# A fused attention and feed-forward kernel: batch 0 loaded on one queue with its values cast on chip, and its first feed-forward units cut by token part

## The chip, the cores and the metric

The kernel runs on one core of a Trainium2 chip. A core has five engines that run their own instruction lists and wait for each other by semaphores: TensorE (PE; its weight loads are shown as PEld), VectorE (DVE), ScalarE (ACT), GpSimd (POOL) and SyncE (SP), which here only issues DMAs. Sixteen DMA engines move the data that the queues of SP, POOL and ACT ask for. The metric is the device time of one execution in microseconds (us).

## The reference

For q, k, v of shape 8 batches x 8 heads x 576 tokens x 64, in float32:

```python
q_s = exp(q - max(q, -1));  q_s /= sum(q_s, -1)        # softmax over the 64 features
k_s = exp(k - max(k, 2));   k_s /= sum(k_s, 2)         # softmax over the 576 tokens
kv  = einsum('bhsd,bhse->bhde', k_s, v)                # 64 x 64 per head
x   = einsum('bhsd,bhde->bhse', q_s, kv)               # -> 4608 rows of 512
g   = x @ w_gate;  u = x @ w_val                       # 512 -> 1536
out = (silu(g) * u) @ w_out                            # 1536 -> 512, float32
```

## The kernel before

**Tiling.** Heads go in two groups G of four (`NG`). One load (`load`, L72) brings a group of q, k or v of one batch as a float32 tile of 128 partitions x 2 x 576 (576 KB). A partition holds nine tokens (`T` = 9) of 64 features, so a group of queries is nine slices t of 64 tokens; `BANKS` cuts them into a part a (t 0 to 4, 320 tokens) and a part b (t 5 to 8, 256 tokens). In what follows "01a" is batch 0, group 1, part a.

**Attention of a group.** ACT takes exponentials of q and k (`exp_of`: tiles `eq`, `ek`). DVE sums the rows of `eq` (`norm_sum`: `rs`, then the reciprocal `rr`) and multiplies (`norm_mul`: `qs`). PE transposes `qs` (`turn_pe`: `tp`), and ACT or DVE copies the result out of PSUM (`turn_out`: `qt`). PE sums the exponentials of the keys over the tokens (`key_sum`: `ks`; DVE takes the reciprocal `kvr`) and multiplies them with the values (`kv_first`: `kv`). ACT or DVE scales that by `kvr` (`scale_first`: `kn`). PE multiplies `qt` with `kn` (`x_mm`: `xp`), and ACT and DVE copy it into the bfloat16 tile `xt` (`x_out`), which the feed-forward part reads. For batch 0 the values arrive in bfloat16 (`v16`): the DMA itself casts them. The later batches are loaded in float32 and cast by GpSimd (`cast_v`).

**Feed-forward.** Twelve units m of 128 columns of `w_gate` and `w_val` (`m_unit`, L286): per unit eight matmuls for gate and eight for value in batch 0, as its 576 tokens are two parts of 320 and 256 columns; ACT applies silu (`sg`), DVE multiplies (`hr`). Output units (`o_mm`, L322) then multiply 128 tokens of `hr` with `w_out`. Batch 0 is fed forward alone, while the loads of batch 1 are awaited; from then on attention of batch b is laid between units of the chunk before it.

**Order of the work.** All engines' orders are written by hand (`manual_schedule`): an engine takes its instructions in the order of the program text. The queue of SP issues the loads of q and k of batch 0, in the order q0, k0, q1, k1. The queue of POOL issues, once k0 has landed, v0, v1 in two pieces, and then the weights in column slices (0 to 256, 256 to 640, 640 to 1024, 1024 to 1536; gate and value in turn, cast from float32 to bfloat16 on the way; `w_slice`, L99) and four slices of `w_out` (`wo_slice`, L107). At most eight DMAs of POOL's queue are outstanding: an issue waits for the one eight before it. The loads of batch 1 (`load_batch`) wait until the second slice of `w_out` has landed. `spin` (L388) runs matmuls on zeros whose result nobody reads, which keep TensorE busy ahead of the real work. `bank` gives out the eight PSUM banks in turn.

**The start, in program order on PE:** 8 spins, 6 spins after the first `rs`, ks0, tp00a, tp00b, 6 spins, ks1, kv0, tp01a, tp01b, x 00a, x 00b, kv1, x 01a, x 01b, and the twelve units, of which the first (`by_part`) does all matmuls of its part of 320 columns before those of 256.

Of the kernel before, what the change touches and what calls it, by code (L numbers as in the profile page):

```python
# [8 lines left out]
FP32 = mybir.dt.float32  # L9
BF16 = mybir.dt.bfloat16  # L10
AF = mybir.ActivationFunctionType
# [4 lines left out]
def kernel(  # L16
# [10 lines left out]
    nc = tc.nc  # L27
# [6 lines left out]
    T = S // 64  # L34
# [12 lines left out]
    def bank(name):  # L47
        return psp.tile([128, 512], FP32, tag="ps", name=name)
# [13 lines left out]

    raw = {}

    def head_ap(src, b, G, t0=0, t1=T):
        return bass.AP(
            tensor=src.tensor,
            offset=src[b, 4 * G].offset + 64 * t0,
            ap=[[T * 64, 128], [2 * HSTR, 2], [1, (t1 - t0) * 64]],
        )  # L70

    def load(what, src, b, G, pieces=((0, T),), after=None):  # L72
        t_ = ld.tile([128, 2, T * 64], FP32, tag=what, name=what)
        raw[what, b, G] = t_
        last = None
        for t0, t1 in pieces:
            last = nc.sync.dma_start(out=t_[:, :, 64 * t0:64 * t1], in_=head_ap(src, b, G, t0, t1))
            if after is not None:
                tc.add_manual_dep(last.ins, after.ins.name, SYNC, reason="order of loads")
                after = None  # L80
        return last
# [37 lines left out]
    def exp_of(what, b, G, pieces=((0, T),)):  # L119
        s = st.setdefault((b, G), {})  # L120
        e = s["e" + what] = at.tile([128, T, 2, 64], BF16, tag="e" + what, name="e" + what)
        src = raw[what, b, G].rearrange("p h (t d) -> p t h d", d=64)
        for t0, t1 in pieces:
            nc.scalar.activation(out=e[:, t0:t1], in_=src[:, t0:t1], func=AF.Exp)  # L124

    def cast_v(b, G):
        nc.gpsimd.tensor_copy(  # L127
# [4 lines left out]
    def norm_sum(b, G, pieces=((0, T),)):  # L132
        s = st[b, G]
        eq2 = s["eq"].rearrange("p t h d -> p (t h) d")
        rs = at.tile([128, 2 * T], FP32, tag="rs", name="rs")
        first = None
        for t0, t1 in pieces:
            i = nc.vector.reduce_sum(  # L138
                out=rs[:, 2 * t0:2 * t1], in_=eq2[:, 2 * t0:2 * t1, :], axis=mybir.AxisListType.X
            )  # L140
            first = first or i
        rr = s["rr"] = at.tile([128, 2 * T], FP32, tag="rr", name="rr")
        nc.vector.reciprocal(out=rr, in_=rs)
        return first

    def norm_mul(b, G, pieces=((0, T),), engs=None):
        s = st[b, G]
        eq2 = s["eq"].rearrange("p t h d -> p (t h) d")
        qs = s["qs"] = at.tile([128, T, 128], BF16, tag="qs", name="qs")
        for (t0, t1), eng in zip(pieces, engs or (nc.vector, nc.vector)):  # L150
            n = 2 * (t1 - t0)
            eng.tensor_mul(  # L152
                qs[:, t0:t1, :].rearrange("p t (h d) -> p (t h) d", d=64),
                eq2[:, 2 * t0:2 * t1, :],
                s["rr"][:, 2 * t0:2 * t1].to_broadcast([128, n, 64]),
            )
# [126 lines left out]

    def m_unit(c0, n, m, by_part=False):  # L286
        ms = slice(m * 128, (m + 1) * 128)
        parts = [(c0, n)] if n <= 512 else [(c0, 320), (c0 + 320, n - 320)]
        gu = []
        for nm in ("g_ps", "u_ps"):  # L290
            ps = [bank(nm) for _ in parts]
            gu.append(ps)
        steps = [(a, kk, i) for a in range(2) for kk in range(KT) for i in range(len(parts))]
        if by_part:
            steps.sort(key=lambda a: (a[2], a[0], a[1]))
        for a, kk, i in steps:
            c, w_ = parts[i]
            nc.tensor.matmul(  # L298
                out=gu[a][i][:, 0:w_], lhsT=(wg, wv)[a][:, kk, ms], rhs=xt[:, kk, c:c + w_],
                start=(kk == 0), stop=(kk == KT - 1),  # L300
            )
        for g_ps, u_ps, (c, w_) in zip(gu[0], gu[1], parts):
            r = c % RING
            sg = ff.tile([128, 512], BF16, tag="sg", name="sg")
            nc.scalar.activation(out=sg[:, 0:w_], in_=g_ps[:, 0:w_], func=AF.Silu)  # L305
            nc.vector.tensor_mul(hr[:, m, r:r + w_], sg[:, 0:w_], u_ps[:, 0:w_])  # L306

    def store(j, o_sb, c0=0, c1=512, engs=(nc.sync, nc.sync)):
        for half in range(2):
# [41 lines left out]

    make_identity(nc, ident)
    with tc.manual_schedule():
        kd = []
        for G in range(NG):
            load("q", q, 0, G)
            kd.append(load("k", k, 0, G))
        d = nc.gpsimd.dma_start(out=v16[0], in_=head_ap(v, 0, 0))
        tc.add_manual_dep(d.ins, kd[0].ins.name, SYNC, reason="order of loads")
        for t0, t1 in BANKS:  # L360
            nc.gpsimd.dma_start(out=v16[1][:, :, 64 * t0:64 * t1], in_=head_ap(v, 0, 1, t0, t1))  # L361

        warm = const.tile([128, 1], FP32, name="warm", tag="warm")
        nc.vector.memset(warm, 0.0)
# [5 lines left out]
        for vb in vbs:  # L370
            nc.vector.memset(vb[:, :, 128:129], 1.0)

        exp_of("q", 0, 0, BANKS)
        exp_of("k", 0, 0)
        exp_of("q", 0, 1, BANKS)
        first = norm_sum(0, 0, BANKS)
        norm_mul(0, 0, BANKS)
        norm_sum(0, 1, BANKS)

        for c0, n in ((0, 256), (256, 384), (640, 384), (1024, 512)):  # L380
            w_slice(wg, moe_w_gate, c0, n)
            w_slice(wv, moe_w_val, c0, n)
        w_dma = [wo_slice(m0, 3) for m0 in (0, 3, 6, 9)]

        def spin(n, after=None):
            idle = bank("idle")
            for _ in range(n):
                i = nc.tensor.matmul(out=idle, lhsT=zero[:, 0:128], rhs=zero, start=True, stop=True)  # L388
                if after is not None:
                    tc.add_manual_dep(i.ins, after.ins.name, SYNC, reason="start of the warm-up")  # L390
                    after = None

        def key_sum(G):
            s = st[0, G]
            ks = bank("ks")
            for t in range(T):
                nc.tensor.matmul(
                    out=ks[:, 0:2], lhsT=s["ek"][:, t, :, :].rearrange("p h d -> p (h d)"), rhs=sel,
                    start=(t == 0), stop=(t == T - 1),
                )  # L400
            s["kvr"] = at.tile([128, 2], FP32, tag="kvr", name="kvr")
            nc.vector.reciprocal(out=s["kvr"], in_=ks[:, 0:2])

        def kv_first(G, t0=0, t1=T):
            s = st[0, G]
            if t0 == 0:
                s["kv"] = [bank("kv") for _ in range(2)]
            for t in range(t0, t1):
                for g in range(2):
                    r = slice(64 * g, 64 * g + 64)  # L410
                    nc.tensor.matmul(
                        out=s["kv"][g][:, 0:128].rearrange("p (h d) -> p h d", d=64),
                        lhsT=ek_of(0, G, g, t), rhs=v16[G][r, :, 64 * t:64 * t + 64],
                        start=(t == 0), stop=(t == T - 1),
                    )

        def scale_first(G, eng1):
            s = st[0, G]
            kn = s["kn"] = at.tile([128, 2, 128], BF16, tag="kn1", name="kn1")
            nc.scalar.mul(kn[:, 0, :], s["kv"][0][:, 0:128], s["kvr"][:, 0:1])  # L420
            if eng1 is nc.scalar:
                nc.scalar.mul(kn[:, 1, :], s["kv"][1][:, 0:128], s["kvr"][:, 1:2])
            else:
                nc.vector.tensor_scalar_mul(kn[:, 1, :], s["kv"][1][:, 0:128], s["kvr"][:, 1:2])

        spin(8)
        spin(6, first)
        key_sum(0)
        turn_pe(0, 0, 0)
        turn_pe(0, 0, 1)  # L430
        turn_out(0, 0, 0, nc.scalar)
        exp_of("k", 0, 1)
        turn_out(0, 0, 1, nc.scalar)
        norm_mul(0, 1, BANKS)
        spin(6)
        key_sum(1)
        kv_first(0)
        scale_first(0, nc.scalar)
        turn_pe(0, 1, 0)
        turn_pe(0, 1, 1)  # L440
        turn_out(0, 1, 0, nc.vector)
        turn_out(0, 1, 1, nc.vector)
        xp0 = x_mm(0, 0, 0), x_mm(0, 0, 1)
        kv_first(1, *BANKS[0])
        kv_first(1, *BANKS[1])
        x_out(0, 0, 0, xp0[0], (nc.scalar, nc.scalar))
        x_out(0, 0, 1, xp0[1], (nc.vector, None))
        scale_first(1, nc.vector)
        xp1 = x_mm(0, 1, 0), x_mm(0, 1, 1)
        x_out(0, 1, 0, xp1[0], (nc.scalar, nc.vector))  # L450
        x_out(0, 0, 1, xp0[1], (None, nc.vector))
        x_out(0, 1, 1, xp1[1], (nc.scalar, nc.vector))

        load_batch(1, w_dma[-3], by_group=True)
        load_batch(2)

        for m in range(MT):
            m_unit(0, S, m, by_part=(m == 0))

        exp_of("q", 1, 0)  # L460
        exp_of("k", 1, 0)
# [121 lines left out]
```

The softmax here doesn't subtract the row's maximum and nothing guards it: scores larger than these inputs give would overflow.

## Time and profile before

| what | value |
|---|---|
| median of 7 runs | 317.46 us (317.23 to 317.70) |
| the profiled execution, its own time | 318.08 us |
| its span, from the first to the last event of the profile | 316.3 us |
| PE busy | 305.8 us (97% of the span) |
| DVE, ACT, POOL busy | 162.9, 147.4, 28.0 us |
| first feed-forward matmul of batch 0 | 14.90 us |
| first output matmul (end of batch 0's units) | 39.60 us |
| mean DMA rate over the span | 145 GB/s |

Times in the traces count from the start of the span. "Busy" of PE is modelled and includes pipelined waiting inside a matmul. The DMA rates count a casting transfer by the bytes that it writes, so the weights, read as float32 and written as bfloat16, show half of what is read. An engine's idle time matters only where it is on the chain that ends last. Nearly all of PE's idle time at the start lies ahead of the first feed-forward matmul and in the first units.

### The profile page before, as it was taken

The numbers are of one execution on the slowest core, as the hardware profiler recorded it, in microseconds if no ns is written. First come the engines' busy times: TensorE is split into PE (matmuls) and PEld (weight loads), VectorE is DVE, ScalarE is ACT, GpSimd is POOL, SyncE is SP. The second block draws the span as 40 slices with busy tenths as digits, with TensorE's granted clock in tenths as the row PEclk, the third lists the DMA queues.
The fourth block names the chain that finished last, engine by engine and source line by source line (L and its number), as shares of the span: only waits on it lengthen the run. The fifth ranks groups of instructions, "written<-read, shape, count | busy, mean of one in ns | idle before, by whom it ended". The sixth has DMA issues, their size and how long they took to land.

```text
span 316.3 us, 4856 instructions
## 1 busy us (share of the span) xinstructions
PE 305.8 (97%) x1865; PEld 152.8 (48%) x1894; DVE 162.9 (52%) x277; ACT 147.4 (47%) x218; POOL 28.0 (9%) x35
## 2 busy tenths in 40 slices
PE   5999999999999999999999999999999999999994
PEld 2577744554445444544454444544454444444443
DVE  3834476685764567455835492639354333423421
ACT  4743397634763465447364647355733113312300
POOL 2920021101100020002000200020000000000000
PEclk9899999999999999999999999999999999999998
DMA  7999999169246906490629253944310202020124
GB/s 270 188 203 207 300 394 390 55 149 373 47 96 168 348 13 132 102 393 21 141 66 347 103 108 69 314 170 102 64 43 0 64 4 66 0 68 3 31 68 102
DMA packets 39304, 45.75 MB, mean 145 GB/s; under 512 B 16368, under 2 KB 23024, under 8 KB 39280
## 3 DMA queue, kind: packets, MB, share of 16 engines
q1 hardware_dynamic: 32480, 39.99, 42.1%
q0 software_dynamic: 6640, 5.31, 10.9%
q8 instruction: 15, 0.25, 0.3%
q10 hardware_dynamic: 160, 0.13, 0.2%
q14 instruction: 9, 0.07, 0.1%
HBM read 37.75 MB, written 9.44 MB: 149 GB/s over the span
## 4 chain that ended last, share of the span: by engine, by line
PE 87%; DMA 5%; DVE 3%; ACT 2%; POOL 1%; issue 1%; SPq 0%; DVEq 0%
PE g_ps L298 28%; PE u_ps L298 28%; PE o_ps L322 25%; DMA wv<-in_moe_w_val_dram 3%; PE kv L191 3%; DMA k<-in_k_dram 2%; DVE rs L138 1%; PE xp L267 1%; DVE qs L152 1%; PE o_ps L342 1%; ACT L124 1%; ACT eq L124 1%; POOL wg L99 0%; POOL v L361 0%; PE tp L166 0%
## 5 line engine op out<-in xcount | busy, mean ns | idle before, releaser
L305 ACT ACTIVATE sg<-g_ps 128x512 bf16<-128x512 f32 (+2 forms) x120 | 65.0, 554 | 139.5 <-PE g_ps L298 120.0
L306 DVE TENSOR_TENSOR hr<-sg,u_ps 128x512 bf16<-128x512 bf16 (+2 forms) x120 | 74.4, 630 | 88.1 <-PE u_ps L298 80.7
L298 PE MATMUL g_ps<-xt,wg 128*128 128x512 bf16 (+2 forms) x469 | 110.0, 357 | 1.0 <-ACT xt L111 0.2
L298 PE MATMUL u_ps<-xt,wv 128*128 128x512 bf16 (+2 forms) x468 | 109.7, 357 | 1.3 <-DMA wv<-in_moe_w_val_dram 0.6
L322 PE MATMUL o_ps<-wo,hr 128*128 128x512 bf16 x414 | 93.0, 379 | 0.4 <-issue 0.2
L298 PEld LDWEIGHTS <-wv 128*128 128x128 bf16 x480 | 46.8, 98 | 47.5 <-DMA wv<-in_moe_w_val_dram 1.3
L298 PEld LDWEIGHTS <-wg 128*128 128x128 bf16 x480 | 45.8, 98 | 45.2 <-issue 1.1
L322 PEld LDWEIGHTS <-hr 128*128 128x128 bf16 x420 | 40.9, 98 | 49.1
L113 DVE COPY o_sb<-o_ps 128x512 f32<-128x512 f32 x33 | 22.4, 680 | 39.2 <-PE o_ps L322 37.3
L127 POOL CAST vb<-v 128x1152 bf16<-128x1152 f32 x14 | 16.0, 1146 | 173.7 <-DMA v<-in_v_dram 166.4
L138 DVE TENSOR_REDUCE rs<-eq 128x18 f32<-128x1152 bf16 (+2 forms) x18 | 21.7, 1214 | 13.0 <-ACT eq L124 13.0
L152 DVE TENSOR_TENSOR qs<-eq,rr 128x1152 bf16<-128x1152 bf16 (+2 forms) x18 | 22.0, 1231 | 0.1
L124 ACT ACTIVATE eq<-q 128x1152 bf16<-128x1152 f32 (+2 forms) x18 | 18.2, 1053 | 4.1 <-DMA q<-in_q_dram 4.0
L124 ACT ACTIVATE ek<-k 128x1152 bf16<-128x1152 f32 x16 | 18.0, 1159 | 0.3 <-DMA k<-in_k_dram 0.2
L305 ACT ACT_TABLE_LOAD x12 | 15.4, 1283 | 0.2
L124 ACT ACT_TABLE_LOAD x11 | 14.1, 1283 | 0.2
L388 PE MATMUL idle<-zero 128*128 128x512 bf16 x20 | 7.3, 526 | 3.2 <-DVE rs L138 2.0
L191 PE MATMUL kv<-vb,ek 64*128 64x129 bf16 x252 | 8.7, 217 | 0.0
L191 PEld LDWEIGHTS <-ek 64*128 64x128 bf16 x252 | 7.3, 94 | 2.7 <-ACT sg L305 2.1
L275 ACT CAST xt<-xp 128x512 bf16<-128x512 f32 x12 | 6.4, 588 | 3.6 <-PE xp L267 3.6
L276 DVE CAST xt<-xp 128x512 bf16<-128x512 f32 x12 | 7.7, 682 | 0.0
L347 ACT COPY o_sb<-o_ps 128x128 f32<-128x128 f32 x2 | 0.5, 266 | 13.3 <-DVE o_sb L346 13.3
(46 smaller groups left out, 71.5 us busy)
## 6 DMA issues: line engine op xcount, KB each, us to landing
q<-in_q_dram SPq DMA_DIRECT2D x16, 576.0 KB, 5.4
k<-in_k_dram SPq DMA_DIRECT2D x16, 576.0 KB, 7.2
out_dram<-o_sb SPq DMA_DIRECT2D x70, 128.0 KB, 2.3
v<-in_v_dram SPq DMA_DIRECT2D x14, 576.0 KB, 8.7
wo<-in_moe_w_out_dram POOLq DMA_DIRECT2D x4, 384.0 KB, 16.7
wg<-in_moe_w_gate_dram POOLq DMA_DIRECT2D x2, 384.0 KB, 10.0
wv<-in_moe_w_val_dram POOLq DMA_DIRECT2D x2, 384.0 KB, 11.1
wg<-in_moe_w_gate_dram POOLq DMA_DIRECT2D x1, 512.0 KB, 14.1
```

What stands on the lines that cost most here:

```text
L113: eng.tensor_copy(out=out, in_=in_)
L124: nc.scalar.activation(out=e[:, t0:t1], in_=src[:, t0:t1], func=AF.Exp)
L127: nc.gpsimd.tensor_copy(out=vbs[G][:, :, 0:128].rearrange("p t (h d) -> p t h d", d=64), in_=raw["v", b, G].rearrange("p h (t d) -> p t h ...
L138: i = nc.vector.reduce_sum(out=rs[:, 2 * t0:2 * t1], in_=eq2[:, 2 * t0:2 * t1, :], axis=mybir.AxisListType.X)
L152: eng.tensor_mul(qs[:, t0:t1, :].rearrange("p t (h d) -> p (t h) d", d=64), eq2[:, 2 * t0:2 * t1, :], s["rr"][:, 2 * t0:2 * t1].to_broadca ...
L191: nc.tensor.matmul(out=kv[g][:, c:c + 129], lhsT=ek_of(b, G, g, t), rhs=vbs[G][r, t, 0:129], start=(t == 0), stop=(t == T - 1),)
L276: nc.vector.tensor_copy(out=xt[:, 2 * G + 1, c0:c0 + 512], in_=main[G][1])
L298: nc.tensor.matmul(out=gu[a][i][:, 0:w_], lhsT=(wg, wv)[a][:, kk, ms], rhs=xt[:, kk, c:c + w_], start=(kk == 0), stop=(kk == KT - 1),)
L305: nc.scalar.activation(out=sg[:, 0:w_], in_=g_ps[:, 0:w_], func=AF.Silu)
L306: nc.vector.tensor_mul(hr[:, m, r:r + w_], sg[:, 0:w_], u_ps[:, 0:w_])
L322: nc.tensor.matmul(out=o_ps, lhsT=hr[:, m, r0:r0 + 128], rhs=wo[:, m, :], start=(m == 0), stop=(m == MT - 1),)
L388: i = nc.tensor.matmul(out=idle, lhsT=zero[:, 0:128], rhs=zero, start=True, stop=True)
```

## The change

- **Loads.** All six loads of batch 0 go to SP's queue in float32, in the order q0, k0, q1, v0, k1, v1, and the first weight DMA waits for v0 in place of v waiting for k0. POOL issues no loads of values.
- **Values** are cast on chip into `v16`: group 0 whole by ACT, group 1 by POOL (t 0 to 2), DVE (t 3 to 5) and ACT (t 6 to 8). POOL's cast stands in its queue between the issue of `wg` 128 to 384 and that of `wv` 128 to 384.
- **Weight slices** are 0 to 128, 128 to 384, 384 to 768, 768 to 1152 and 1152 to 1536: ten DMAs in place of eight, for the same bytes.
- **Query normalization** is done part by part (`norm_part`: sum, reciprocal, product), and part 01b is left until the feed-forward has begun.
- **Key sums of group 1** are taken in two parts, and ACT's exponentials of k1 come in two pieces, after the cast of v0. The scaling of `kv` is done by DVE twice for group 0, and by ACT and DVE for group 1.
- **The first three units** are split by `m_part` and `m_out`: matmuls of units 0, 1 and 2 on the first 320 tokens, with tp01b after unit 1 and x 01b after unit 2, and then of units 0, 1, 2 on the other 256.
- **Spins:** 10, and three times 3, tied to the first exponential, the first row sum and the first reciprocal; 3 more before tp00b and 6 before tp01a.

```diff
-        kd = []
-        for G in range(NG):
-            load("q", q, 0, G)
-            kd.append(load("k", k, 0, G))
-        d = nc.gpsimd.dma_start(out=v16[0], in_=head_ap(v, 0, 0))
-        tc.add_manual_dep(d.ins, kd[0].ins.name, SYNC, reason="order of loads")
-        for t0, t1 in BANKS:
-            nc.gpsimd.dma_start(out=v16[1][:, :, 64 * t0:64 * t1], in_=head_ap(v, 0, 1, t0, t1))
+        for what, src, G in (("q", q, 0), ("k", k, 0), ("q", q, 1), ("v", v, 0), ("k", k, 1), ("v", v, 1)):
+            d = load(what, src, 0, G)
+            if (what, G) == ("v", 0):
+                v_dma = d
...
+        steps += norm_part(0, 0)
+        norm_part(0, 1)
+        def cast_part(G, eng, t0, t1):
+            c = slice(64 * t0, 64 * t1)
+            copy(eng, v16[G][:, :, c], raw["v", 0, G][:, :, c])
+        w0 = w_slice(wg, moe_w_gate, 0, 128)
+        tc.add_manual_dep(w0.ins, v_dma.ins.name, SYNC, reason="order of loads")
+        w_slice(wv, moe_w_val, 0, 128)
+        w_slice(wg, moe_w_gate, 128, 256)
+        cast_part(1, nc.gpsimd, 0, 3)
+        w_slice(wv, moe_w_val, 128, 256)
-        for c0, n in ((0, 256), (256, 384), (640, 384), (1024, 512)):
+        for c0, n in ((384, 384), (768, 384), (1152, 384)):
...
-        spin(8)
-        spin(6, first)
-        key_sum(0)
-        turn_pe(0, 0, 0)
+        spin(10)
+        for i in (0, 2, 3):
+            spin(3, steps[i])
+        turn_pe(0, 0, 0)
+        turn_out(0, 0, 0, nc.scalar)
+        exp_of("q", 0, 1, BANKS)
+        key_sum(0)
+        spin(3)
         turn_pe(0, 0, 1)
-        turn_out(0, 0, 0, nc.scalar)
-        exp_of("k", 0, 1)
         turn_out(0, 0, 1, nc.scalar)
-        norm_mul(0, 1, BANKS)
+        norm_part(1, 0)
+        cast_part(0, nc.scalar, 0, T)
         spin(6)
-        key_sum(1)
+        turn_pe(0, 1, 0)
+        turn_out(0, 1, 0, nc.vector)
+        exp_of("k", 0, 1, BANKS)
+        key_rec(0)
         kv_first(0)
-        scale_first(0, nc.scalar)
...
+        scale_first(0, (nc.vector, nc.vector))
+        key_sum(1, *BANKS[0])
+        cast_part(1, nc.vector, 3, 6)
+        cast_part(1, nc.scalar, 6, T)
+        xp = x_mm(0, 0, 0)
+        key_sum(1, *BANKS[1])
+        kv_first(1)
+        x_out(0, 0, 0, xp)
+        key_rec(1)
+        scale_first(1, (nc.scalar, nc.vector))
+        xp = x_mm(0, 1, 0), x_mm(0, 0, 1)
+        x_out(0, 1, 0, xp[0])
+        x_out(0, 0, 1, xp[1])
+        half = (0, 320), (320, S - 320)
+        units = [m_part(0, half[:1], m) for m in range(2)]
+        norm_part(1, 1)
         turn_pe(0, 1, 1)
+        units.append(m_part(0, half[:1], 2))
+        m_out(units[0])
         turn_out(0, 1, 1, nc.vector)
...
+        m_out(units[1])
+        x_out(0, 1, 1, x_mm(0, 1, 1))
+        m_out(units[2])
+        for m in range(3):
+            m_out(m_part(0, half[1:], m))
...
-        for m in range(MT):
-            m_unit(0, S, m, by_part=(m == 0))
+        for m in range(3, MT):
+            m_unit(0, S, m)
```

## The prediction

> **What bounds the kernel now.** The page's chain by engine comes first, then the chain in order of time, the timeline of the first 40 us, and the busy time by stretches for DMA and clock.
>
> ```profile
> PE 87%; DMA 5%; DVE 3%; ACT 2%; POOL 1%; issue 1%; SPq 0%; DVEq 0%
> ```
>
> TensorE carries the span; what can be won or lost here is the 13% beside it. In order of time, much of that lies at the start:
>
> ```profile
> 1.26 4.96 DMA k<-in_k_dram
> ...
> 11.01 9.91 DMA wv<-in_moe_w_val_dram
> 20.93 0.04 issue
> 20.97 1.15 PE u_ps L298 x8
> 22.13 0.98 PE g_ps L298 x8
> ```
>
> Up to 20.97 the chain runs through loads, POOL's issues and a weight slice; from there PE has no gap until batch 0's units are over. The timeline shows what PE did before:
>
> ```profile
> 1.22 3.20 PE L388 MATMUL idle<-zero 128*128 128x512 bf16 x8 [1.22 <-DVE sel L367]
> ...
> 8.27 1.26 ACT L124 ACTIVATE eq<-q 128x640 bf16<-128x640 f32 x2 [0.86 <-DMA q<-in_q_dram]
> ...
> 9.43 0.67 ACT L111 COPY qt<-tp 128x640 bf16<-128x640 bf16 x1
> ...
> 14.51 0.45 PE L220 MATMUL xp<-qt,kn 64*64 64x320 bf16 x8 [0.45 <-DVE kn L424]
> ...
> 14.90 0.90 PE L298 MATMUL g_ps<-xt,wg 128*128 128x320 bf16 x4
> ...
> 16.00 0.72 PE L298 MATMUL u_ps<-xt,wv 128*128 128x320 bf16 x4 [0.20 <-DMA wv<-in_moe_w_val_dram]
> ...
> 20.97 1.15 PE L298 MATMUL u_ps<-xt,wv 128*128 128x320 bf16 x8 [0.44 <-DMA wv<-in_moe_w_val_dram]
> ...
> 39.60 5.34 PE L322 MATMUL o_ps<-wo,hr 128*128 128x512 bf16 x23
> ```
>
> Units start at 14.90 and output matmuls at 39.60: 24.70 us. Twelve units at 2 x 0.98 are 23.52; the other 1.18 are waits, nearly all for `wv`. So two things decide: when the units start, and when the weights land.
>
> ```profile
> 2.00:8.00 6.00, 3.98 (x13) 1.47 (x12) 2.38 (x4) 2.64 (x5) 1.47 (x2) 0.94 0.98 359
> 8.00:11.00 3.00, 3.00 (x24) 1.89 (x23) 2.65 (x7) 2.73 (x4) 3.00 (x5) 0.55 1.15 204
> 11.00:14.00 3.00, 3.00 (x65) 2.13 (x62) 2.48 (x6) 1.90 (x6) 3.00 (x6) 1.00 1.29 164
> 16.00:24.00 8.00, 7.56 (x61) 5.87 (x62) 2.54 (x7) 3.73 (x9) 2.32 (x3) 1.00 1.31 204
> ```
>
> The last column is GB/s, the one two before it the granted clock. Cast transfers count what they write, so 164 and 204 are 328 and 408 read: the DMA engines are full from 2 us on, and the stretch with 1 KB rows (values and the first slices) is a fifth slower than that with 1.5 KB rows.
>
> **The sum is made at the end of batch 0's units.** Behind it PE is filled, and batch 1's first exponentials follow the last silu on ACT (39.05, table load 39.44, `eq` 40.74), so a later end moves the whole rest. An earlier end does not wholly: `eq` of q(1,1) waits for its load until 43.58, its `qs` is ready at 48.97, and its transposes begin at 49.34. Only 0.37 us can be won there unless batch 1's loads, queued behind all weights, come earlier too.
>
> **Loads.** A load of 0.59 MB takes 1.5 us at the 390 GB/s of the seconds from 6 to 8. q0 and k0 land as before (4.75, 6.2). q1 no longer shares the engines with v: 7.7 in place of 8.25. v0 follows at 9.2, k1 at 10.7, v1 at 12.2 to 13, as weights join. POOL issued 0.30 us after k0's landing; so the first weight issue is at 9.5, and three issues at 0.8 end at 11.9.
>
> **New wait on POOL.** The cast of t 0 to 2 then waits for v1 (0.3 to 1.1 us) and runs 0.4 (a third of `vb`'s 1.15). Queued behind it are `wv` 128 to 384 and all later slices: issued at 12.7 to 13.4. That slice ends 5.11 MB into the stream (six loads 3.54, weights 1.57). Before, 4.59 MB (`wv` 0 to 256) had landed at 15.96 and 5.38 MB (`wg` 256 to 640) by 19.4; between them 5.11 MB falls at 18.2. At 390 GB/s from 2 us on, with the 0.8 us by which landings trailed the first loads, it would be 15.9. I take 17.7, nearer the row that has landings.
>
> The Trainium skill speaks against the new slices here: "DMA: Bandwidth & Descriptors", Specifications, asks for 512 B or more per transfer, below which the engine reads, modifies and writes. The slices of 128 columns write rows of 256 B. Should that halve their rate, by my estimate from this page their 0.52 MB would take 1.3 us more, and the sum below would be 1.3 us higher. The trace of before has no such rows; its own trend (328 against 408) speaks for a few tenths, which lie inside the bounds taken.
>
> **When the units start.** `eq` 00a ends at 5.53. DVE: `rs` 0.78, `rr` 0.2 (between 0.14 for 2 and 0.27 for 18 elements), `qs` 0.83: 7.4. PE must first end its spins: ten at 0.43 end at 5.5, then three threes. Before, 4.2 us passed between the second burst's start (6.43) and the fall of a weight load from 0.15 to 0.10 us, with the clock column at 0.55 meanwhile. Busy from 1.2 on, PE would be fast at 5.4 and tp00a starts at 7.4; if it stays slow through all nine, at 9.4. I take 8.0, nearer the first, as the clock followed unbroken work in the trace.
>
> From here ACT's list is the path: `qt` 00a 0.67, `eq` 01 1.25, `qt` 00b 0.57, cast of v0 1.16 (the price of an `ek` of the same shape), `ek` 01 1.25, cast of a third of v1 0.43 (as a 320-wide `xt`): 5.33, from 8.45 to 13.8. Beside it: cast of v0 done 12.1, kv0 0.68, two `kn` by DVE 0.35 each, done 13.6; x 00a and the rest of ks1 0.5: 14.05. DVE's `rs`, `rr`, `qs` of 01a end at 11.7, and the transposes fit before kv0. DVE's cast of v1, with no row of its kind, is 0.2 to 0.45 (`xt` of 256 from PSUM is 0.42) and ends by 14.05 either way. Then kv1 0.68, `kn` 0.45 with its hand-over, x 01a and x 00b 0.5: units start at 15.7, against 14.90. Bounds: tp00a at 7.4 gives 15.1, at 9.4 it gives 17.1. The durations of one engine overlap a little (two `eq` of 0.74 and 0.61 took 1.26); over the list that may take another 0.5 off.
>
> **In the units.** tp01b (4 of 9 transposes, 0.3) and x 01b (0.2) now stand between units: 0.5 that before came ahead of them. DVE's rest of 01b (0.68, 0.2, 0.69) starts after the copies at 16.3 and ends at 17.9, about when unit 1 is over: nothing. `wv` 128 to 384 is wanted at 15.7 + 1.08 + 0.54 = 17.3 and lands at 17.7: 0.4, bounds 0 and 0.9. Units on 256 columns wait for ACT's and DVE's copy of x 01b: 0.4 less two matmuls of 0.11, so about 0.3, where silu 0 and 1 on ACT, past the table load of 1.28, do not hold it. Later slices have over 2 us to spare. In place of 1.18, 0.5 + 0.4 + 0.3 = 1.2. The changed spins and key sums have no price outside the path above.
>
> End: 15.7 + 23.52 + 1.2 = 40.4, that is 0.8 later. Batch 1's loads may come up to 1.2 us later before they add to that; the same bytes go through the same engines, so I add nothing.
>
> The profiled execution took 318.08 (span 316.3 and 1.78 around it); it becomes 318.9. The runs' median is 0.62 below it: 317.46 + 0.8 = 318.3.
>
> **Rivals.**
> - *Faster: the start is shorter than the list.* For it: q1 lands 0.55 earlier, PE is warm for tp00a, the values no longer pass the casting queue that moved only 328 GB/s, and overlaps take 0.5 off ACT. Units then start at 14.6, `wv` is there, waits are 0.3 and moved work 0.5: end 38.9, -0.7, and with batch 1's loads earlier by the freed DMA time nearly all of it arrives: 316.7 to 316.8. It decides when the units start before 14.7. Against it: ACT has 1.6 us of casts more, and takes `eq` 01 only after `qt` 00a.
> - *No difference:* start at 15.2, waits 0.5, moved work 0.5: end 39.7, +0.1: 317.6.
> - *Much slower: `wv` 128 to 384 behind the cast on POOL.* If v1 lands after 13.5 or the short rows run slowly, the slice lands at 19: 19.0, then 22.5 of work and waits: 41.5, +1.9: 319.4. tp00a at 9.4 alone gives nearly as much: 17.1 + 23.52 + 0.8 = 41.4.
>
> **How the numbers follow.** This kernel's measurement can tell about 0.2%, 0.63 us. My forecast (start 15.3 to 16.4, +0.63 to +1.6) has 0.47, its own range 318.1 to 319.1; much slower 0.10; no difference 0.25; faster 0.18. So slower 0.57, same 0.25, faster 0.18. The range runs from the faster case to the much slower one, 316.7 to 319.5; what lies beyond either is under 2 in 10.
>
> **What would show it.** Right: the first unit's matmul between 15.3 and 16.4, ACT without gap from about 8.5 to its last cast, PE waiting for `wv` in unit 1, output matmuls from 40.0 to 41.2. Wrong: units before 14.9, PE idle in front of tp00a beyond 8.5, or `wv` landed before 17; also a wait for q(1,1) that grows past 1 us, since then the loads and not the units carry the loss.

## The result and the profile after

The changed kernel takes 319.79 us (median of 12 runs; 319.77 without the one of 657.02 us) and the kernel before 317.46 us (31 runs): a ratio of 1.0081, 95% interval 1.0065 to 1.0097. It is slower by 2.33 us. The forecast was 318.3, so the direction held and the size came out nearly three times as large; the time lies 0.3 us above the range.

In the execution that was profiled first TensorE ran at half speed from end to end (told in the last section), so the profile after is that of a second job with the same kernel. Its profiled execution took 320.2 us, with a span of 318.4 us, 2.1 us more than the profiled execution before on both counts.

The chain that ended last in the changed kernel (start, duration, what), in order of time up to the point where part 01b enters the units:

```profile
3.29 9.34 DMA v<-in_v_dram
12.63 0.05 issue
12.69 0.45 POOL v L113
13.14 5.90 DMA wv<-in_moe_w_val_dram
19.04 0.05 issue
19.09 0.72 PE u_ps L293 x4
...
21.40 0.37 ACT xt L111
```

The path to the first units no longer runs through the loads of k. It runs through v1, the last load on SP's queue, then GpSimd's cast of it, then the weight slice `wv` 128 to 384 whose issue stood behind that cast. The timeline of the changed kernel has the same three steps from the engines' side, with the idle time ahead of an instruction and its releaser in brackets:

```profile
7.56 0.44 PE L167 MATMUL tp<-ident,qs 128*128 128x128 bf16 x5
...
12.69 0.50 POOL L113 CAST v<-v 128x384 bf16<-128x384 f32 x1 [0.59 <-DMA v<-in_v_dram]
...
13.14 0.75 POOL L99 DMA_DIRECT2D wv<-in_moe_w_val_dram  x1
...
15.19 0.90 PE L293 MATMUL g_ps<-xt,wg 128*128 128x320 bf16 x4
...
16.48 0.72 PE L293 MATMUL g_ps<-xt,wg 128*128 128x320 bf16 x4
...
19.09 0.72 PE L293 MATMUL u_ps<-xt,wv 128*128 128x320 bf16 x4 [1.89 <-DMA wv<-in_moe_w_val_dram]
...
41.85 5.34 PE L325 MATMUL o_ps<-wo,hr 128*128 128x512 bf16 x23
```

The units start at 15.19, 0.29 later than before. Unit 1's gate matmuls follow unit 0 without a gap, and then PE stands until its value slice is there. The output matmuls begin at 41.85 in place of 39.60: 2.25 us later, which is nearly the whole loss of 2.33.

A matmul group's duration in the timeline runs some 0.18 us past the point where the next group can start (groups of four matmuls of 320 columns follow each other every 0.54, and the row says 0.72). So the value matmuls of unit 1 were wanted at 16.48 + 0.54 = 17.02, and began 2.07 us later. With that the stretch from 15.19 to 41.85 closes: 23.52 of matmuls, 2.07 for `wv`, 0.46 for the moved transposes and x 01b, 0.2 in the first gate group (the next group follows it after 0.73 in place of 0.54) and 0.4 around the first matmuls on part 01b, most of it (0.3) for the copy of their `xt` by ACT and DVE: 26.65, against 26.66 read.

The busy time by stretches, with the clock, DMA share and GB/s in the last three columns, first of the changed kernel:

```profile
2.00:8.00 6.00, 5.83 (x30) 2.31 (x29) 2.52 (x5) 2.65 (x5) 0.00 (x0) 1.00 0.99 356
8.00:11.00 3.00, 2.57 (x23) 0.99 (x18) 2.36 (x5) 2.96 (x5) 1.30 (x2) 1.00 1.03 396
11.00:14.00 3.00, 2.30 (x48) 1.69 (x50) 2.16 (x7) 2.50 (x5) 2.40 (x5) 1.00 1.20 156
14.00:16.00 2.00, 1.52 (x27) 0.81 (x22) 1.33 (x6) 1.18 (x5) 2.00 (x3) 1.00 1.21 154
16.00:18.00 2.00, 1.20 (x9) 0.53 (x7) 1.86 (x5) 1.94 (x3) 2.00 (x4) 1.00 1.34 175
16.00:24.00 8.00, 5.97 (x52) 4.12 (x51) 4.55 (x11) 3.44 (x8) 5.37 (x8) 1.00 1.30 190
```

and of the kernel before, with the issue that the failed step below is measured against:

```profile
14.00:16.00 2.00, 1.32 (x16) 0.47 (x13) 1.43 (x4) 1.55 (x5) 1.51 (x3) 1.00 1.36 193
16.00:18.00 2.00, 2.00 (x17) 1.66 (x18) 0.71 (x3) 1.60 (x3) 0.77 (x1) 1.00 1.31 205
```

```profile
9.55 0.78 POOL L99 DMA_DIRECT2D wv<-in_moe_w_val_dram  x1
```

The float32 loads keep the engines at 356 to 396 GB/s until 11 us. The last of them, v1, ends at 12.63, and from then on only casting transfers are left. The rate is 156 from 11 to 14 us and later 190, where before it was 164 and 204. Weights were issued later and also arrived more slowly for a while.

### The profile page after: what moved, and what is told of

It reads as the page before. It is cut to its first block, busy times and chain, and to the rows that moved or that the text cites. A ratio compares the mean times of both kernels' runs of the same rounds, so it can differ in the third digit from the quotient of the medians.

```text
span 655.2 us, 4878 instructions
## 1 busy us (share of the span) xinstructions
PE 642.0 (98%) x1873; PEld 232.7 (36%) x1902; DVE 168.2 (26%) x282; ACT 149.4 (23%) x219; POOL 27.8 (4%) x35
## 4 chain that ended last, share of the span: by engine, by line
PE 97%; issue 1%; DMA 1%; DVE 0%; SPq 0%; ACT 0%
PE g_ps L293 30%; PE u_ps L293 30%; PE o_ps L325 30%; PE idle L415 2%; PE kv L192 2%; PE xp L268 1%; PE o_ps L345 1%; DMA q<-in_q_dram 1%; PE tp L167 1%; PE xp L221 0%; PE kv L441 0%; SPq L319 0%; DVE o_sb L113 0%; PE ks L425 0%; ACT kn L453 0%
## 5 line engine op out<-in xcount | busy, mean ns | idle before, releaser
L293 PE MATMUL u_ps<-xt,wv 128*128 128x512 bf16 (+3 forms) x468 | 221.3, 635 | 3.0 <-issue 3.0
L293 PE MATMUL g_ps<-xt,wg 128*128 128x512 bf16 (+3 forms) x469 | 219.5, 628 | 3.2 <-issue 3.0
L325 PE MATMUL o_ps<-wo,hr 128*128 128x512 bf16 x414 | 198.1, 682 | 1.2 <-issue 1.2
L304 ACT ACTIVATE sg<-g_ps 128x512 bf16<-128x512 f32 (+3 forms) x120 | 65.6, 554 | 430.7 <-PE g_ps L293 395.3
L305 DVE TENSOR_TENSOR hr<-sg,u_ps 128x512 bf16<-128x512 bf16 (+3 forms) x120 | 75.4, 634 | 298.8 <-PE u_ps L293 283.1
L293 PEld LDWEIGHTS <-wv 128*128 128x128 bf16 x480 | 71.4, 149 | 130.9 <-issue 120.4
L293 PEld LDWEIGHTS <-wg 128*128 128x128 bf16 x480 | 69.4, 147 | 122.0 <-issue 111.6
L325 PEld LDWEIGHTS <-hr 128*128 128x128 bf16 x420 | 62.3, 149 | 132.2 <-issue 131.4
L138 DVE TENSOR_REDUCE rs<-eq 128x18 f32<-128x1152 bf16 x14 | 18.9, 1348 | 2.5 <-ACT eq L124 2.5
L153 DVE TENSOR_TENSOR qs<-eq,rr 128x1152 bf16<-128x1152 bf16 x14 | 19.1, 1365 | 0.0
L192 PEld LDWEIGHTS <-ek 64*128 64x128 bf16 x252 | 12.7, 131 | 6.2 <-issue 5.7
## 6 DMA issues: line engine op xcount, KB each, us to landing
wo<-in_moe_w_out_dram POOLq DMA_DIRECT2D x4, 384.0 KB, 15.2
wv<-in_moe_w_val_dram POOLq DMA_DIRECT2D x3, 384.0 KB, 11.4
```

The costliest lines, as they stand in the source:

```text
L138: nc.vector.reduce_sum(out=rs[:, 2 * t0:2 * t1], in_=eq2[:, 2 * t0:2 * t1, :], axis=mybir.AxisListType.X)
L153: nc.vector.tensor_mul(qs[:, t0:t1, :].rearrange("p t (h d) -> p (t h) d", d=64), eq2[:, 2 * t0:2 * t1, :], s["rr"][:, 2 * t0:2 * t1].to_b ...
L192: nc.tensor.matmul(out=kv[g][:, c:c + 129], lhsT=ek_of(b, G, g, t), rhs=vbs[G][r, t, 0:129], start=(t == 0), stop=(t == T - 1),)
L293: nc.tensor.matmul(out=ps[:, 0:w_], lhsT=(wg, wv)[a][:, kk, ms], rhs=xt[:, kk, c:c + w_], start=(kk == 0), stop=(kk == KT - 1),)
L325: nc.tensor.matmul(out=o_ps, lhsT=hr[:, m, r0:r0 + 128], rhs=wo[:, m, :], start=(m == 0), stop=(m == MT - 1),)
```

## The experiments

The question is which part makes PE wait 2.07 us for one slice: the slices' shape, GpSimd's cast ahead of the issue, the late first weight issue, the spins, or the order of the units, which wants the slice sooner. All were timed in five rounds, in three jobs, each beside the kernel before (medians 317.53, 317.42 and 317.51); a ratio is always to the kernel before of the same job.

### The changed kernel again

> The changed kernel again. Theory W (weights): the slice wv 128 to 384 lands at about 19, PE waits for it in unit 1 for over 1 us, and batch 0's units end about 22.7 us after it, near 41.5 to 42; +2 to +2.5 us against before. Theory S (start): the units start at 16.5 or later with wv already there, ACT's list being late, and the end is the start plus 24.7; the same +2 would need a start at 16.9. Theory C (clock): PE stays at half its clock for longer at the start (tp00a near 9.5 to 10) and S follows from that.

Measured: 320.19 us, ratio 1.0076 [1.0063, 1.0090]. It is the profile shown above. The wait for `wv` alone, 2.07 us, is nearly the size of the loss.

### Wide slices in the changed kernel

```diff
-        w0 = w_slice(wg, moe_w_gate, 0, 128)
+        w0 = w_slice(wg, moe_w_gate, 0, 256)
-        w_slice(wv, moe_w_val, 0, 128)
-        w_slice(wg, moe_w_gate, 128, 256)
+        w_slice(wv, moe_w_val, 0, 256)
+        w_slice(wg, moe_w_gate, 256, 384)
         cast_part(1, nc.gpsimd, 0, 3)
-        w_slice(wv, moe_w_val, 128, 256)
-        for c0, n in ((384, 384), (768, 384), (1152, 384)):
+        w_slice(wv, moe_w_val, 256, 384)
+        for c0, n in ((640, 384), (1024, 512)):
```

> The changed kernel with the weight slices of before (0 to 256, 256 to 640, 640 to 1024, 1024 to 1536) and POOL's cast still between the third and the fourth issue. Theory W, if rows of 128 and 256 columns slow the stream: batch 1's loads start near 33.7 in place of 35.2, units 0 and 1 find their weights, unit 2 waits to about 21, and the time falls by 0.8 to 1.5 us against the changed kernel. If the rows are not it: landings of the same bytes stay late, and the time rises by up to 1 us, since unit 2's weights are then the 6.16th MB in place of the 5.11th. Theories S and C: the start of the units is unchanged and so is the end, within 0.4.

Measured: 323.05 us, ratio 1.0172 [1.0158, 1.0186], the slowest of all. The timeline shows three waits in place of one, the last two in unit 2:

```profile
16.77 0.72 PE L293 MATMUL u_ps<-xt,wv 128*128 128x320 bf16 x4 [0.60 <-DMA wv<-in_moe_w_val_dram]
...
19.49 0.72 PE L293 MATMUL g_ps<-xt,wg 128*128 128x320 bf16 x4 [0.69 <-DMA wg<-in_moe_w_gate_dram]
...
21.40 0.86 PE L293 MATMUL u_ps<-xt,wv 128*128 128x320 bf16 x4 [1.19 <-DMA wv<-in_moe_w_val_dram]
```

The granted clock was 0.73 in the stretch from 20 to 24 and 0.84 from 24 to 28, so some of the loss is clock and not waiting. The narrow slices help this order of units; they are not what costs.

### Narrow slices in the kernel before

```diff
-        for c0, n in ((0, 256), (256, 384), (640, 384), (1024, 512)):
+        for c0, n in ((0, 128), (128, 256), (384, 384), (768, 384), (1152, 384)):
```

> The kernel before with only the weight slices of the change (0 to 128, 128 to 384, then three of 384), its loads and order kept. Theory W by rows: the weights end 1 to 1.4 us later than in before, units wait for them, and the time is 0.8 to 1.5 us above before. If the short rows are harmless: within 0.3 us of before, or a little faster, as unit 0's weights come in smaller slices.

Measured: 318.22 us, ratio 1.0018 [1.0009, 1.0027], between the two expectations, although in the profiled execution no unit waited for a weight and the output matmuls began at 39.06, 0.54 earlier than before. That execution took 317.76 us, one of four between 317.74 and 317.78; the other seven took 318.20 to 318.56, and no profile shows what they lost. Of the 0.54 in the profile, about half was lost behind the units. The chain that ended last in this kernel has, among its longest pieces:

```profile
34.92 8.66 DMA q<-in_q_dram
...
44.80 1.36 DVE rs L138
...
47.33 1.68 DVE qs L152
```

This is the load of q(1,1). Its exponentials began at 43.61 (43.58 before), and PE's transposes of that group at 49.06 in place of 49.34. So 0.28 us of the earlier end arrived, which fits the limit of 0.37 that the prediction had named: an earlier end of batch 0's units gives little unless batch 1's loads are earlier too.

### The spins

```diff
-        spin(10)
-        for i in (0, 2, 3):
-            spin(3, steps[i])
+        spin(8)
+        spin(6, steps[2])
```

> The changed kernel with the spins at the start as in before (8, a pause, 6 after the first row sum). Theory C: the clock opens as in before at 10 to 10.7, tp00a starts near 9, and the time falls by up to 1 us if the start decides. Theory W: the end stays where wv's landing puts it, within 0.3 us of the changed kernel, wherever the units start.

Measured: 320.19 us, ratio 1.0080 [1.0068, 1.0093]: no change against the changed kernel. But its parts moved. tp00a came at 8.69 in place of 7.56 and the units started 1.4 us later, and yet the output matmuls came no later. The timeline (of the fastest of its five executions, 319.60 us):

```profile
16.60 0.90 PE L293 MATMUL g_ps<-xt,wg 128*128 128x320 bf16 x4
...
18.42 0.71 PE L293 MATMUL u_ps<-xt,wv 128*128 128x320 bf16 x4
...
41.28 5.34 PE L325 MATMUL o_ps<-wo,hr 128*128 128x512 bf16 x23
```

Unit 1's value matmuls begin with no wait at 18.42, so the slice had landed by then. The units took 24.68 us: 23.52, 0.46, 0.2, 0.4 and 0.1 of rest, the sum from above without the term for `wv`. So the start of the units does not set their end in the changed kernel. What PE saves ahead of unit 0 it waits for in unit 1.

### GpSimd's cast given to DVE, or put later

```diff
# one kernel
-        cast_part(1, nc.gpsimd, 0, 3)
-        cast_part(1, nc.vector, 3, 6)
+        cast_part(1, nc.vector, 0, 6)
# the other
-        cast_part(1, nc.gpsimd, 0, 3)
         w_slice(wv, moe_w_val, 128, 256)
+        cast_part(1, nc.gpsimd, 0, 3)
```

> The changed kernel with POOL's third of the cast of v1 given to DVE, which then casts t 0 to 5 (0.3 us more on DVE). POOL waits for nothing between its weight issues, so wv 128 to 384 is issued at 12.1 in place of 13.1. Theory Q (the queue behind the cast): the slice lands at 18.0 in place of 19.04, PE's wait in unit 1 falls from 1.9 to 0.9, and the time falls by 0.9 to 1.1 us against the changed kernel (to about 319.1). Theory P (place in the byte stream): the engines had work in hand, the slice lands where its bytes come, at 18.7 to 19.1, and the time stays within 0.3 us.

> The changed kernel with POOL's cast moved behind the issue of wv 128 to 384, ahead of wg 384 to 768. Theory Q: the same fall as with the cast on DVE, 0.9 to 1.1 us, while the later slices keep their lateness and batch 1's loads still start near 34.5; their slack of over 2 us hides it. Theory P: within 0.3 us of the changed kernel.

Measured: 319.84 us, ratio 1.0069 [1.0045, 1.0093], and 319.60 us, ratio 1.0073 [1.0044, 1.0102]. By the times alone neither is told apart from the changed kernel. The profiles do tell something. The issue of `wv` 128 to 384 came at 12.09 and 12.63 in place of 13.14, and the slice landed at 18.41 and 18.49 in place of 19.04. With the first:

```profile
15.66 0.90 PE L293 MATMUL g_ps<-xt,wg 128*128 128x320 bf16 x4
...
18.46 0.72 PE L293 MATMUL u_ps<-xt,wv 128*128 128x320 bf16 x4 [0.63 <-DMA wv<-in_moe_w_val_dram]
```

The wait in the row fell from 1.89 to 0.63, half of it because unit 1 asked later (its gate matmuls began at 17.11 in place of 16.48). At the output matmuls a gain of 0.6 us is left in the first and 0.5 in the second (41.23, 41.31 against 41.85). In the second the loads themselves came later (first weight issue at 10.27 in place of 9.70), so this one does not price the move of the cast alone. The cast in POOL's queue makes the slice land some 0.6 us later, a little over half of the 1.04 that theory Q had said, and that is about a quarter of the loss by the profiles; the times do not confirm it.

### Weights started after q1

This kernel also has the cast put later, as above.

```diff
         for what, src, G in (("q", q, 0), ("k", k, 0), ("q", q, 1), ("v", v, 0), ("k", k, 1), ("v", v, 1)):
             d = load(what, src, 0, G)
-            if (what, G) == ("v", 0):
+            if (what, G) == ("q", 1):
                 v_dma = d
```

> As the one before (POOL's cast behind wv 128 to 384), and the first weight DMA waits for q1 in place of v0: issued at 8.3 in place of 9.7. Theory Q: wv 128 to 384 lands another 1 us earlier, at 17, when PE wants it (17.1), and the wait in unit 1 goes; v1, which now shares the engines, lands 0.5 to 1 us later, so the units start 0.2 to 0.8 later. Together 0 to 0.8 us below the kernel before this one, 318.3 to 319. Theory P: little change, as the order of the bytes alone moves.

Measured: 318.46 us, ratio 1.0021 [1.0002, 1.0041]. Over half of the loss is gone: 1.04 us are left of 2.33, in the profiles 0.93 of 2.25 at the output matmuls. The timeline:

```profile
8.20 0.90 POOL L99 DMA_DIRECT2D wg<-in_moe_w_gate_dram  x1 [6.90 <-DMA q<-in_q_dram]
...
10.57 0.77 POOL L99 DMA_DIRECT2D wv<-in_moe_w_val_dram  x1
...
15.84 0.90 PE L293 MATMUL g_ps<-xt,wg 128*128 128x320 bf16 x4
...
17.66 0.71 PE L293 MATMUL u_ps<-xt,wv 128*128 128x320 bf16 x4
...
40.53 5.34 PE L325 MATMUL o_ps<-wo,hr 128*128 128x512 bf16 x24
```

The first weight issue is 1.5 us earlier than in the changed kernel, four weight transfers are queued before v1 is even awaited, and PE waits for no slice. The units take 24.69 us, the same as before (24.70): what the wait for `wv` cost the old order, the moved work costs this one. The units start 0.94 later than before, the output matmuls 0.93 later, and the median is 1.04 us higher. So what is left here is a later start. Much of it is the profiled execution's own, which took 318.87 us: its spins ran longer, and tp00a came at 8.22, 0.66 later than in the changed kernel's profile. With the same spins it came at 7.56, 8.01 and 7.48 in the profiles of the changed kernel and of the two kernels with the cast moved. The changed kernel's own loss of 2.25 us is 0.29 of later start and 1.96 more in the units.

### Narrow slices before, with batch 1's loads released one slice sooner

```diff
-        for c0, n in ((0, 256), (256, 384), (640, 384), (1024, 512)):
+        for c0, n in ((0, 128), (128, 256), (384, 384), (768, 384), (1152, 384)):
-        load_batch(1, w_dma[-3], by_group=True)
+        load_batch(1, w_dma[-4], by_group=True)
```

> The kernel before with the thin weight slices, and with batch 1's loads waiting for the first slice of w_out in place of the second. With thin slices alone the units ended at 39.06, 0.54 before those of the kernel before, but q(1,1) came too late for that to arrive. If that load is what holds it: the load comes 1 to 2 us earlier, the gain arrives, and the time is 0.3 to 0.6 us below the kernel before. If not: as with thin slices alone, 0 to 0.7 us above it.

Measured: 317.98 us, ratio 1.0014 [0.9997, 1.0031]: no gain. The loads did start earlier (32.63 against 33.73), but in the profiled execution, at 319.00 the longest of its twelve, unit 3 waited 0.75 us for `wv` and the output matmuls came at 39.65. This is inconclusive as to what the freed limit is worth, since the units' end was not earlier in the run that was seen. No kernel of this study beats the kernel before.

### Part 01b not left for later

```diff
         cast_part(1, nc.scalar, 6, T)
+        norm_part(1, 1)
...
+        turn_pe(0, 1, 1)
         x_out(0, 1, 0, xp[0])
+        turn_out(0, 1, 1, nc.scalar)
...
-        units = [m_part(0, half[:1], m) for m in range(2)]
-        norm_part(1, 1)
-        turn_pe(0, 1, 1)
-        units.append(m_part(0, half[:1], 2))
...
+        unit = m_part(0, half[:1], 0)
         x_out(0, 1, 1, x_mm(0, 1, 1))
-        m_out(units[2])
-        for m in range(3):
-            m_out(m_part(0, half[1:], m))
+        m_out(unit)
+        m_out(m_part(0, half[1:], 0))
...
-        for m in range(3, MT):
+        for m in range(1, MT):
```

One kernel has this edit alone, the other has it on top of the weights started after q1.

> The changed kernel with part 01b not left for later: DVE normalizes it after its cast of v1, its transposes and copies come ahead of or within unit 0, and the units run as in before (unit 0 by part, then whole). Theory D (demand): running units 0 to 2 on 320 tokens first asks for wv 128 to 384 after 1.6 us of units in place of 2.9, so the split spends the weights sooner than they land. Then without it the units start later, at 16 to 16.5, wv is there when wanted at 19, and the units end at 40 to 40.4: 1.3 to 1.8 us below the changed kernel, 318.3 to 318.9. Theory Q/W alone (the slices are late, whatever the order): the wait stays near 1 us or more and the time is within 0.5 us of the changed kernel.

> As the one before, with the first weight waiting for q1 and POOL's cast behind wv 128 to 384. Theory D: the weights are no longer late by then, so nothing more is won: 318 to 318.8, and its units start at 16.3 to 16.8 as v1 comes later. If weights still held it: 0.5 to 1 us less than the one before.

Measured: 320.79 us, ratio 1.0097 [1.0082, 1.0113], and 321.16 us, ratio 1.0102 [1.0073, 1.0131]. Both are slower than expected. No unit waited for a weight, but the time was lost in two other places. The timeline of the first:

```profile
14.61 0.69 DVE L388 TENSOR_TENSOR qs<-eq,rr 128x512 bf16<-128x512 bf16 x1
...
15.62 0.16 DVE L433 RECIPROCAL kvr<-ks 128x2 f32<-128x2 f32 x1
...
15.88 0.37 ACT L453 ACTIVATE kn<-kv,kvr 128x128 bf16<-128x128 f32 x1 [1.57 <-DVE kvr L433]
...
17.08 1.27 PE L293 MATMUL g_ps<-xt,wg 128*128 128x320 bf16 x4
```

DVE's normalization of 01b, which ends with `qs` here, now stands ahead of the reciprocal of the key sums. So `kn` of group 1 comes at 15.88 in place of 14.38, tp01b stands ahead of unit 0, and the units start 1.9 later (17.08). PE had nothing to do from 14.65 to 16.30, and then the clock fell; busy time by stretches of the same kernel:

```profile
14.00:16.00 2.00, 0.65 (x20) 0.47 (x18) 1.82 (x6) 0.43 (x2) 2.00 (x4) 1.00 0.97 108
16.00:18.00 2.00, 1.70 (x16) 1.12 (x17) 1.06 (x3) 1.35 (x4) 2.00 (x4) 0.65 1.23 143
18.00:20.00 2.00, 2.00 (x12) 0.85 (x11) 0.14 (x1) 0.36 (x2) 1.96 (x3) 0.50 1.15 168
```

In these two kernels the first unit ran at half speed in the profile. So they do not price the order of the units cleanly. The executions whose mean clock is given as 1.00 (one of five, two of six) took 319.68, and 319.26 and 319.19 us, which is still 1.7 to 2.2 us above the kernel before. What the profiles show is that leaving 01b for later is what kept the change's start at 15.2 to 15.8.

### The kernel before with only its first units split

```diff
-        for m in range(MT):
-            m_unit(0, S, m, by_part=(m == 0))
+        for c, w in ((0, 320), (320, S - 320)):
+            for m in range(3):
+                m_unit(c, w, m)
+        for m in range(3, MT):
+            m_unit(0, S, m)
```

Loads, casts, slices, spins and normalization are those of the kernel before; only units 0, 1 and 2 run first on 320 and then on 256 tokens.

> The kernel before with only its first three units cut by token part: units 0, 1, 2 on 320 tokens, then on 256; all else kept. Theory D: unit 2's value slice, the second one of wv, which lands at 20.9, is now wanted at about 17.7, so PE waits about 3 us in place of 0.4 and the units end near 41.7: +2 us against before, 319.4 to 319.8, or more should PE's clock fall in that wait. If the demand is not it: no change within 0.3 us, since the matmuls are the same ones.

Measured: 319.83 us, ratio 1.0079 [1.0058, 1.0101], as much as the whole change. The timeline:

```profile
15.20 0.90 PE L298 MATMUL g_ps<-xt,wg 128*128 128x320 bf16 x4
...
20.28 0.72 PE L298 MATMUL u_ps<-xt,wv 128*128 128x320 bf16 x4 [1.99 <-DMA wv<-in_moe_w_val_dram]
...
41.10 5.34 PE L322 MATMUL o_ps<-wo,hr 128*128 128x512 bf16 x23
```

The slice `wv` 256 to 640 was issued at 10.90, in the same place as before, and landed at 20.2. Before, unit 2's value matmuls asked for it at about 20.4. In the split order unit 2 asks after five groups of 0.54 and the 0.2 of the first: at 18.10, and it waits 2.18 us (again 0.18 more than the bracket says). 23.52 + 2.18 + 0.2 is 25.90, just the stretch from 15.20 to 41.10.

## Why the prediction was right in direction and wrong in size

Here is each step against the changed kernel's profile.

- **Loads and POOL's issues: right.** v1 was there at 12.63 (forecast 12.2 to 13), the first weight issue at 9.70 (9.5), the issue behind the cast at 13.14 (12.7 to 13.4).
- **Start of the units: inside its bounds, but outside its own range.** tp00a came at 7.56, near the lower bound of 7.4: the spins were over when DVE's product was ready. The units started at 15.19, in place of 15.7; by itself this error made the forecast end 0.5 too late. There is luck in the 7.56: the nineteen spins took 6.50 us here and 7.16 in the early-weight run, where tp00a came at 8.22.
- **The landing of `wv` 128 to 384: the step that failed.** It was the term "lands at 17.7: 0.4, bounds 0 and 0.9". The slice landed at 19.04, and with the earlier start the wait was 2.07. That PE would wait for this slice in unit 1 was right; the size was not. The slice's place in the stream of bytes was priced at the rate of the kernel before. But here less arrived: from 11 to 18 us 156, 154 and 175 GB/s were written in stretches of 3, 2 and 2 us, 1.13 MB in all, of which 0.92 MB came through the casting queue and most of the rest is the end of v1; before, 164, 193 and 205 made 1.29 MB, nearly all through the casting queue. And POOL could not issue the slice before 13.14, from where it took 5.90. A row of before had that price: `wv` 0 to 256, issued at 9.55 and landed at 15.96, took 6.41, which from 12.7 to 13.4 gives 19.1 to 19.8. The 17.7 taken by place and this reading by time from issue lay 1.4 us and more apart, and only the first entered the bounds of the wait.
- **What of before's 1.18 was weights: slightly misread.** Some 0.2 of it stood in the first gate group, which every kernel here has, and should have stayed in the sum. The copy of `xt` 01b cost 0.4 (forecast 0.3), the moved work 0.46 (0.5).
- **Everything behind follows: right.** Start -0.51, wait +1.67, first gate +0.2, copy +0.1, moved work -0.04 make +1.42, and the end came at 41.85 where 40.4 was forecast. The time followed the end of the units: 2.25 us there, 2.1 in the spans, 2.33 in the medians. Batch 1's loads were issued at 34.51, 0.78 later, inside the 1.2 that were said to cost nothing.
- **The rivals.** What happened is the "much slower" one, which had said 19.0 for the landing, 41.5 for the end and 319.4 for the time, but had been given a chance of 0.10. Its numbers came out better than its reasons. Its conditions were v1 after 13.5, and v1 landed at 12.63, or slow short rows, of which the runs show a few tenths (below). It put the lateness down to the cast on POOL, and the profiles give that 0.6 us of landing. The early-weight run shows the larger part: with the cast already moved, the earlier first issue took another 1.1 us off the median (319.60 to 318.46), so the first issue, tied to v0, was too late for this order. The split alone in the kernel before shows the other half of the same thing, which the forecast had passed over in one clause ("wanted at 15.7 + 1.08 + 0.54"): the split brings the demand for the second slice forward, and it costs 2 us even with the old supply.
- **Short rows.** The Trainium skill, "DMA: Bandwidth & Descriptors", Specifications, speaks against transfers below 512 B. Halving, which would have cost 1.3 us by the prediction's estimate, did not come. With the narrow slices in the kernel before, the microsecond from 12 to 13 had 652 of its 679 packets (the pieces in which the profile counts a transfer) below 512 B and wrote 176 GB/s, against 171 before, with 12 of 345 short. But from 13 to 14, with 310 of 420 packets short, it wrote 131 against 186, and from 11 to 18 us 1.21 MB against 1.29. That is 0.4 us at the 200 GB/s of the stretches behind it, an estimate, and near the few tenths that the prediction had read from the trend. That trend was no clean price of rows itself: within its stretch from 11 to 14 us the kernel before rose from 135 over 171 to 186. No unit waited for a weight in the run with narrow slices.

What stays open is why the casting queue wrote less in the changed kernel. Between 13 and 14 us it wrote 90 GB/s, and 189 in the early-weight run, where four weight transfers had been queued by 11.4. Short rows are a part of this: 264 of 314 packets of that microsecond were below 512 B in the changed kernel, 46 of 395 in the other. They are not all of it: from 14 to 18 us, with 81 of 1222 packets short, the changed kernel wrote 164 GB/s and the early-weight run 193. That fewer outstanding transfers are the reason would fit, but no run isolates it.

## What to carry to other kernels

An order that starts consumers on half of their data also asks for the next weights in little more than half the time: work out when each slice is wanted under the new order, before counting what the earlier start brings. Price the landing of a transfer in two ways, from its place among the bytes and from its issue by a measured issue-to-landing time, and where they disagree let the range hold both. An engine's instruction placed in a queue that also issues DMAs delays every issue behind it by its wait as well as by its own time: here 13.14 in place of 12.09.

## What was not expected of the hardware

One execution of the changed kernel, of 657.02 us, ran with TensorE at half speed for all of its span of 655.2 us, with PE busy 98% of it. The same group of the page's costliest groups, first there (busy, mean ns), then in the other execution:

```profile
L325 PE MATMUL o_ps<-wo,hr 128*128 128x512 bf16 x414 | 198.1, 682 | 1.2 <-issue 1.2
```

```profile
L325 PE MATMUL o_ps<-wo,hr 128*128 128x512 bf16 x414 | 93.0, 379 | 0.4 <-issue 0.2
```

Weight loads took 149 ns in place of 98, and the other engines were as fast as ever. The clock's record says 1.00 all through, so here only the durations tell. It was one of 12 executions, and its cause is open.

The clock also fell after short pauses: to 0.50 in the run with 01b ahead of the units, where the longest wait of PE that the timeline shows is 1.66 us, and not at all in the changed kernel after 1.89 us. "TensorE: Matmul & The Clock Gate" of the Trainium skill (Part 1) has the clock return to half after an idle window of about 3.4 us. No single pause here was that long, so that rule alone does not say when the clock will fall. Nor does the busy share of PE just before: 0.65 of 2 us (14 to 16) in the run where it fell, 0.20 of 2 us (17 to 19) in the changed kernel, where it did not. Over 3.4 us it tells no more: 1.43 us up to 16.30 in the run where it fell, and 1.41 us up to 20.28 in the kernel before with split units, where it stayed at 1.00.
